# One-core attention and feed-forward kernel: the front recorded by the clocked loop with another load order, the tail in interleaved halves, the last key tile split, V products that may wait in the queue

## Chip, core and metric

The kernel runs on one core of one Trainium2 chip. The metric is the device time of one execution in microseconds. TensorE (PE), VectorE (DVE), ScalarE (ACT), GpSimd (POOL) and SyncE (SP) each take their instructions in order and meet at semaphores.

## What is computed

One token stream x of 2048 rows by 512 is normalised. Attention with 32 query heads of width 16 over one shared key and value head, and a feed-forward block of width 1792, both read the normalised rows; the second gates the first.

```python
xn = _layernorm(x, axis=-1)
q = (xn @ wq).reshape(B, S, 32, 16).transpose(0, 2, 1, 3)
k = xn @ wk
v = xn @ wv
p = softmax(einsum("bhqd,bkd->bhqk", q, k) * 16 ** -0.5)
s = einsum("bhqk,bkd->bhqd", p, v).transpose(0, 2, 1, 3).reshape(B, S, 512) @ wo
g = _silu(einsum("bsf,fd->bsd", _silu(xn @ w1), w2))
out = x + s * g
```

## The kernel before

Queries are cut into 4 chunks of 512, heads into 8 groups of 4: 32 groups, each against 16 key tiles of 128. One block is one head's scores of 512 queries against one key tile; a group has 64, all have 2048. `burst` (scores, L577) lets TensorE multiply blocks of a tile side by side in its row groups, from keys in `kTa_sb` for even groups and in `kTb_sb` for odd ones, where `move_K` (L430) copies them by DMA.

A block is exponentiated in one of two ways. Way A, `exp_A` (L606): two blocks stand in one of two PSUM buffers, `psA0` or `psA1`, and one ScalarE instruction takes both, 1024 columns. Way D, `exp_D` (L628): VectorE turns one bank (`D`, `D1` or `F`) into int16 bit patterns of an approximate exponential; when the four blocks of a tile are done, GpSimd adds two constants (L639), which gives three approximations of each block. So a block of way A needs one V product and one of way D three, with weighted copies of V (`vaug_sb`, L445). V products (`emit_PV`, L676) gather in the bank `psO`, four heads side by side. After a group's last one VectorE reads `psO` out with a transpose (`gn1`, L709), takes reciprocals of the sums (L717), scales (L726) and, every second group, transposes back (L736). Only then may the next group's V products write `psO`.

Dense work fills TensorE between score bursts: Q products, the feed-forward (`h` and `z`, whose ScalarE tanh is L882) and the output projection, with jobs planned over the run (L844). Weights are `w1_sb`, `w2_sb`, `wop_sb`.

The order is written by a recorder, `Sched`: each `op` gets its semaphore waits and advances a model of each engine's clock. From the thirteenth key tile on, a loop asks these clocks which instruction comes next: a score burst as late as ScalarE allows, V products or dense work ahead of it, filler matmuls (L865) where modelled TensorE activity is below `KEEP`. The front is written out by hand. For x tiles 0 to 3: statistics (L338), aggregates (L341), epsilon added (L352), Sqrt on ScalarE (L354), reciprocal (L355), the bias -mean x rstd (L359), normalisation on three engines (L366, L369), TensorE transposes and their evictions (L397 to L404), the first 128 keys (L412, L422), the Exp table (L484), Q of the first two groups (L454, L464), the other keys of chunk 0 (L424). Then 12 key tiles of group 0, all in way A, with the other three x chunks' work at fixed places (`dve_pre`, `pe_pre`); there rstd is taken on GpSimd by a power (L345, L347), and `warm` adds matmuls of zeros (L329). SyncE's queue issues most loads, K copies, x reloads and output stores; w1 and w2 are issued from GpSimd's (L323, L324).

The tail: the last four output tiles gather in `psA0` and `psA1` (L1163), first their share of the other groups by an identity matmul, then the last pair of groups. VectorE gates two of them (L1176); ScalarE copies two (L1179), which VectorE gates (L1183); it adds x to each (L893), and four stores leave, three from SyncE's queue and one from ScalarE's.

Of the kernel before, what the change touches and what calls it, by code (L numbers as in the profile page):

```python
# [6 lines left out]
ALU = mybir.AluOpType  # L7
# [25 lines left out]
PSUM_KEYS = {"A0", "A1", "D", "D1", "O", "F"}  # L33
# [163 lines left out]
def bass_recurrent_scan__grouped_kv_mqa__dense_activation_silu__prompt_kernel(  # L197
# [30 lines left out]
    NWARM2 = 2  # L228
    NWARM3 = 2
    NFRONT = 12  # L230
    AGE2 = 12.0
    KEEP, ENDQ, ROUND, MAXJOB, AHEAD, Q_EARLY = 0.6, 12, 3.0, 2, 3, 0.20
    LEAD, LEAD_END, SLIP, AGE, AGE1, MARGIN = 3, 3, 0.15, 2.0, 1.2, 0.0
    NF, F_FROM, F_LEFT, F_LATE, DENSE_END, HOLD, F_BEHIND = 14, 0.05, 9, 3, 0.95, 10, 0

    with ExitStack() as es:
# [32 lines left out]
        nb_sb = sb("nb_sb", [P, NT], FP32)  # L269
# [23 lines left out]
        def load_x(a, b, queue="sp"):  # L293
            op(queue, lambda e: e.dma_start(x_sb[:, a:b, :], xv[:, a:b, :]), writes=[("x", t) for t in range(a, b)],
               lane=f"lx{a}", cost=2.0 if b - a == 1 else 5.0)
# [5 lines left out]
        op("sp", lambda e: e.dma_start(wkn_sb[:], A_wk.rearrange("(dc p) e -> p dc e", p=P)), writes=["wkn"], lane="lwk")  # L301
        load_x(4, 8)
        op("sp", lambda e: e.dma_start(wq_sb[:], A_wq.rearrange("(dc p) n -> p dc n", p=P)), writes=["wq"], lane="lwq", cost=8.0)
        op("sp", lambda e: e.dma_start(wv_sb[:], A_wv.rearrange("(dc p) e -> p dc e", p=P)), writes=["wv"], lane="lwv")
# [6 lines left out]
        op("gp", lambda e: e.memset(mhalf_sb[:], -0.5), writes=["mhalf"])  # L311
        op("gp", lambda e: e.memset(scr_i[:], 0), writes=["scri"])
        op("v", lambda e: e.memset(zero_sb[:], 0.0), writes=["zero"])

# [5 lines left out]

        def late_loads():
            op("sp", lambda e: e.dma_start(wop_sb[:], A_wo.rearrange("(t p) n -> p t n", p=P)), writes=["wop"], lane="lwo")
            op("gp", lambda e: e.dma_start(w1_sb[:], B_w1.rearrange("(dc p) f -> p dc f", p=P)), writes=["w1"], lane="lw1")  # L323
            op("gp", lambda e: e.dma_start(w2_sb[:], B_w2.rearrange("(ft p) n -> p ft n", p=P)), writes=["w2"], lane="lw2")  # L324
# [12 lines left out]
        def stats(t):  # L337
            op("v", lambda e: e.bn_stats(stats_sb[:, t, :], x_sb[:, t, :]), reads=[("x", t)], writes=[("st", t)])  # L338

        def aggr(t):  # L340
            op("v", lambda e: e.bn_aggr(mv_sb[:, t, :], stats_sb[:, t, :]), reads=[("st", t)], writes=[("mv", t)])  # L341
# [8 lines left out]
        def rstd_sqrt(c):  # L350
            sl = slice(4 * c, 4 * c + 4)
            op("v", lambda e: e.tensor_scalar(rstd_sb[:, sl], mv_sb[:, sl, 1], LN_EPS, None, op0=ALU.add),  # L352
               reads=[("mv", t) for t in tiles(c)], writes=[("rstd", c)])
            op("a", lambda e: e.activation(rstd_sb[:, sl], rstd_sb[:, sl], ACT.Sqrt), reads=[("rstd", c)], writes=[("rstd", c)])  # L354
            op("v", lambda e: e.reciprocal(rstd_sb[:, sl], rstd_sb[:, sl]), reads=[("rstd", c)], writes=[("rstd", c)])  # L355

        def nbias(c):
            sl = slice(4 * c, 4 * c + 4)
            op("v", lambda e: e.scalar_tensor_tensor(out=nb_sb[:, sl], in0=mv_sb[:, sl, 0], scalar=-1.0, in1=rstd_sb[:, sl],  # L359
                                                     op0=ALU.mult, op1=ALU.mult),  # L360
               reads=[("mv", t) for t in tiles(c)] + [("rstd", c)], writes=[("nb", c)])

        def normalise(t, eng):
            rd = [("x", t), ("rstd", t // 4), ("nb", t // 4)]
            if eng == "a":
                op("a", lambda e: e.activation(xn_sb[:, t % 8, :], x_sb[:, t, :], ACT.Identity, bias=nb_sb[:, t:t + 1],  # L366
                                               scale=rstd_sb[:, t:t + 1]), reads=rd, writes=[("xn", t % 8)])
# [856 lines left out]
```

## Time and profile before

| what | us |
|---|---|
| median of three runs (683.57 to 683.84) | 683.79 |
| the profiled execution | 684.74 |
| its span, first to last instruction | 682.9 |
| first exponential of way A starts | 11.84 |
| last one ends | 673.68 |
| last group of V products (start and length) | 673.74, 0.40 |
| ScalarE, VectorE, TensorE busy | 665.0, 589.6, 640.3 |

The span is that of the profiled execution, not of the median run; what lies outside it is 1.8 us. Times in the trace count from the span's start. A row of the timeline merges equal instructions without a gap: its start, its length, their number, and in brackets the idle time before it with what ended that. Rows of a windows view give a stretch, its length, the busy time of PE, PE's weight loads, DVE, ACT and POOL with the number of instructions, then the granted TensorE clock as a share of full speed, the DMA share and GB/s.

### The profile page before, as it was taken

The numbers are of one execution on the slowest core, as the hardware profiler recorded it, in microseconds if no ns is written. First come the engines' busy times: TensorE is split into PE (matmuls) and PEld (weight loads), VectorE is DVE, ScalarE is ACT, GpSimd is POOL, SyncE is SP. The second block draws the span as 40 slices with busy tenths as digits, with TensorE's granted clock in tenths as the row PEclk, the third lists the DMA queues.
The fourth block names the chain that finished last, engine by engine and source line by source line (L and its number), as shares of the span: only waits on it lengthen the run. The fifth ranks groups of instructions, "written<-read, shape, count | busy, mean of one in ns | idle before, by whom it ended". The sixth has DMA issues, their size and how long they took to land.

```text
span 682.9 us, 14794 instructions
## 1 busy us (share of the span) xinstructions
PE 640.3 (94%) x6224; PEld 185.9 (27%) x6303; DVE 589.6 (86%) x976; ACT 665.0 (97%) x759; POOL 369.3 (54%) x375
## 2 busy tenths in 40 slices
PE   8999999999999999999999999999999999999986
PEld 3432222222222222222222222222222222222222
DVE  7788888779898889988888898998898989889985
ACT  5999999999999999999999999999999999999995
POOL 5134554456565556465564565556555556756553
PEclk9999999999999999999999999999999999999999
DMA  8310000000000001000000000000000000000100
GB/s 296 119 36 1 1 2 1 1 1 2 1 1 1 2 16 32 16 3 1 1 1 2 2 1 1 17 17 16 18 1 1 1 1 2 1 2 16 48 1 32
DMA packets 10194, 12.25 MB, mean 18 GB/s; under 512 B 2000, under 2 KB 9424, under 8 KB 10128
## 3 DMA queue, kind: packets, MB, share of 16 engines
q1 hardware_dynamic: 8960, 7.25, 3.6%
q0 software_dynamic: 736, 3.67, 1.5%
q8 instruction: 49, 0.80, 0.5%
q10 hardware_dynamic: 432, 0.39, 0.2%
q14 instruction: 17, 0.14, 0.1%
HBM read 8.95 MB, written 2.10 MB: 16 GB/s over the span
## 4 chain that ended last, share of the span: by engine, by line
ACT 88%; PE 7%; DVE 3%; DMA 0%; POOL 0%; issue 0%; DVEq 0%
ACT pa_sb L606 83%; ACT t_sb L882 5%; PE psA L577 2%; PE psO L676 2%; DVE stats_sb L338 1%; PE psF L844 1%; PE psF L329 0%; DVE ph_sb L628 0%; DMA x_sb<-in_A_x_dram 0%; PE psD L377 0%; DVE xn_sb L369 0%; POOL rstd_sb L347 0%; PE psD L412 0%; PE psF L412 0%; DVE kTa_sb L424 0%
## 5 line engine op out<-in xcount | busy, mean ns | idle before, releaser
L606 ACT ACTIVATE pa_sb<-psA 128x1024 bf16<-128x1024 f32 x678 | 644.4, 1189 | 3.9 <-PE psA L577 2.0
L639 POOL INT64_ADD ph_sb<-ph_sb x260 | 268.7, 1046 | 214.6 <-DVE ph_sb L628 214.6
L628 DVE TENSOR_SCALAR ph_sb<-psD 128x512 int16<-128x512 f32 (+1 forms) x464 | 321.9, 703 | 49.8 <-PE psD L577 41.3
L676 PE MATMUL psO<-ph_sb,vaug_sb 128*32 128x512 bf16 x1560 | 204.0, 385 | 0.4 <-ACT pa_sb L606 0.2
L676 PE MATMUL psO<-pa_sb,vaug_sb 128*32 128x512 bf16 x1356 | 202.9, 385 | 0.6 <-DVE vaug_sb L445 0.3
L577 PE MATMUL psA<-qT_sb,kTa_sb 32*128 32x512 bf16 x692 | 134.2, 384 | 10.2 <-ACT pa_sb L606 7.0
L577 PE MATMUL psA<-qT_sb,kTb_sb 32*128 32x512 bf16 x664 | 129.2, 386 | 11.8 <-ACT pa_sb L606 9.8
L639 POOL INT64_ADD x_sb<-x_sb x86 | 89.0, 1047 | 63.1 <-DVE x_sb L628 63.1
L577 PE MATMUL psD<-qT_sb,kTb_sb 32*128 32x512 bf16 x327 | 120.1, 386 | 0.4 <-DVE ph_sb L628 0.4
L628 DVE TENSOR_SCALAR x_sb<-psD 128x512 int16<-128x512 f32 (+1 forms) x149 | 104.0, 702 | 15.2 <-PE psD L577 14.0
L577 PE MATMUL psD<-qT_sb,kTa_sb 32*128 32x512 bf16 x309 | 112.0, 384 | 0.0
L676 PE MATMUL psO<-x_sb,vaug_sb 128*32 128x512 bf16 x516 | 92.9, 386 | 0.1
L577 PEld LDWEIGHTS psA<-qT_sb,kTa_sb 32*128 32x128 bf16 x692 | 32.5, 91 | 141.8 <-ACT pa_sb L606 129.0
L577 PEld LDWEIGHTS psA<-qT_sb,kTb_sb 32*128 32x128 bf16 x664 | 31.2, 91 | 144.5 <-ACT pa_sb L606 132.9
L676 PEld LDWEIGHTS psO<-ph_sb,vaug_sb 128*32 128x32 bf16 x1560 | 51.7, 95 | 50.7 <-issue 33.1
L844 PE MATMUL psF<-xnT_sb,w_sb 128*128 128x512 bf16 x194 | 60.9, 384 | 3.9 <-issue 2.4
L844 PE MATMUL psF<-w_sb,u_sb 128*128 128x512 bf16 x205 | 61.3, 383 | 2.5 <-issue 1.9
L676 PEld LDWEIGHTS psO<-pa_sb,vaug_sb 128*32 128x32 bf16 x1356 | 50.8, 94 | 45.2 <-issue 30.1
L882 ACT ACTIVATE t_sb<-psF 128x512 bf16<-128x512 f32 x72 | 55.2, 766 | 0.0
L914 DVE SCALAR_TENSOR_TENSOR u_sb<-t_sb,psF 128x512 bf16<-128x512 bf16 x56 | 38.3, 683 | 8.3 <-ACT t_sb L882 7.8
L577 PEld LDWEIGHTS psD<-qT_sb,kTb_sb 32*128 32x128 bf16 x327 | 28.3, 91 | 0.9 <-DVE ph_sb L628 0.7
L676 PEld LDWEIGHTS psO<-x_sb,vaug_sb 128*32 128x32 bf16 x516 | 23.1, 95 | 16.0 <-issue 11.2
(98 smaller groups left out, 361.1 us busy)
## 6 DMA issues: line engine op xcount, KB each, us to landing
w_sb<-in_B_w_dram POOLq DMA_DIRECT2D x2, 1792.0 KB, 12.3
x_sb<-in_A_x_dram SPq DMA_DIRECT2D x18, 128.0 KB, 2.3
out_dram<-ob_sb SPq DMA_DIRECT2D x15, 128.0 KB, 1.7
x_sb<-in_A_x_dram SPq DMA_DIRECT2D x3, 512.0 KB, 6.9
wq_sb<-in_A_wq_dram SPq DMA_DIRECT2D x1, 512.0 KB, 6.4
wop_sb<-in_A_wo_dram SPq DMA_DIRECT2D x1, 512.0 KB, 10.1
x_sb<-in_A_x_dram ACTq DMA_DIRECT2D x2, 128.0 KB, 3.1
kTb_sb<-kTa_sb SPq DMA_DIRECT2D x16, 16.0 KB, 2.9
```

Source lines behind the costliest of these rows:

```text
L338: op("v", lambda e: e.bn_stats(stats_sb[:, t, :], x_sb[:, t, :]), reads=[("x", t)], writes=[("st", t)])
L577: return e.matmul(ap, lhsT=kT_sb[g % 2][32 * i:32 * i + 32, kt * P:(kt + 1) * P], rhs=qT_sb[32 * i:32 * i + 32, c % 2, g // 2, :], start=T ...
L606: d = op("a", lambda e: e.activation(pa_sb[:, sl, :], psA[k][:, :], ACT.Exp, scale=ESCALE), reads=["A%d" % k], writes=[("pa", sl)], cost=2 ...
L628: d = op("v", lambda e: e.tensor_scalar(ph_ap(0, sl, 512 * pos, 512 * pos + m), src, float(PH_ONE + PH_BIAS), 0.0, op0=ALU.add, op1=ALU.ma ...
L639: d = op("gp", lambda e, j=j: e.int64_add(ph_ap(j, sl, 0, 2048).bitcast(I64), ph_ap(0, sl, 0, 2048).bitcast(I64), PH_SHIFT[j] * 0x00010001 ...
L676: r = e.matmul(psO[32 * i:32 * i + 32, :], lhsT=vaug_sb[:, p["v"], p["kt"], :], rhs=p["ap"], start=s0, stop=s1, tile_position=(0, 32 * i), ...
L844: h = e.matmul(ap, lhsT=l, rhs=r, start=(m == 0), stop=(m == end))
L882: op("a", lambda e: e.activation(t_sb[:, n % 2, :], bank_ap(b), ACT.Tanh, scale=0.5 if jb[0] == "h" else 0.25), reads=[b], writes=[("t", n ...
L914: op("v", lambda e: e.scalar_tensor_tensor(out=dst, in0=t_sb[:, n % 2, :], scalar=1.0, in1=src, op0=ALU.add, op1=ALU.mult), reads=tk["read ...
```

## The change

- Front: Sqrt takes epsilon as its bias, the Exp table is loaded right behind it, normalisation subtracts the mean itself and runs on VectorE alone. Evictions of the first transposes alternate between VectorE and ScalarE. First Q is computed in four pieces of 128 columns, evicted in two of 256 on ScalarE. The first 128 columns of wq have a load of their own, ahead of x tiles 4 to 7; w1 and w2 are loaded from SyncE's queue, w1 behind the K copies of chunk 0, w2 behind those of chunk 3.
- The hand-written list of 12 tiles is gone. Statistics, aggregates, normalisations become tasks of VectorE in the loop; transposes, K and V products of the x chunks become front jobs, which the loop places when their inputs are modelled ready and a bank is free. Way D may start for group 1 while the front runs. The three ph buffers and the one in x tiles are chosen by which is free.
- V products of a group may be queued up to `PVWAIT` before the modelled end of the last group's readout.
- In the last group one key tile is split: two of its blocks go way A, two way D, whose two additions run on VectorE.
- Tail: readout, reciprocal, scaling and back transpose run in halves of 256 columns, one half behind the other; each of the four output tiles has its own key. TensorE adds x and the gated product for tiles 0 and 2 in `psD`; ScalarE copies and stores them.

```diff
--- before
+++ after
-    NWARM2 = 2
+    NWARM2 = 0
...
-    LEAD, LEAD_END, SLIP, AGE, AGE1, MARGIN = 3, 3, 0.15, 2.0, 1.2, 0.0
+    LEAD, LEAD_END, SLIP, AGE, AGE1, MARGIN = 3, 3, 0.2, 2.0, 1.2, 0.0
+    HALF_LO, HALF_HI = 1, 3
+    EV = "vava"
+    PVWAIT = 0.2
...
+        wqv = A_wq.rearrange("(dc p) n -> p dc n", p=P)
+        op("sp", lambda e: e.dma_start(wq_sb[:, :, 0:P], wqv[:, :, 0:P]), writes=["wq0"], lane="lwq0", cost=4.0)
         load_x(4, 8)
-        op("sp", lambda e: e.dma_start(wq_sb[:], A_wq.rearrange("(dc p) n -> p dc n", p=P)), writes=["wq"], lane="lwq", cost=8.0)
-        op("sp", lambda e: e.dma_start(wv_sb[:], A_wv.rearrange("(dc p) e -> p dc e", p=P)), writes=["wv"], lane="lwv")
+        op("sp", lambda e: e.dma_start(wq_sb[:, :, P:D], wqv[:, :, P:D]), writes=["wq"], lane="lwq", cost=5.0)
+        op("sp", lambda e: e.dma_start(wv_sb[:], A_wv.rearrange("(dc p) e -> p dc e", p=P)), writes=["wv"], lane="lwv", cost=5.0)
...
+        def load_w1():
+            op("sp", lambda e: e.dma_start(w1_sb[:], B_w1.rearrange("(dc p) f -> p dc f", p=P)), writes=["w1"], lane="lw1", cost=7.0)
+
         def late_loads():
-            op("sp", lambda e: e.dma_start(wop_sb[:], A_wo.rearrange("(t p) n -> p t n", p=P)), writes=["wop"], lane="lwo")
-            op("gp", lambda e: e.dma_start(w1_sb[:], B_w1.rearrange("(dc p) f -> p dc f", p=P)), writes=["w1"], lane="lw1")
-            op("gp", lambda e: e.dma_start(w2_sb[:], B_w2.rearrange("(ft p) n -> p ft n", p=P)), writes=["w2"], lane="lw2")
+            op("sp", lambda e: e.dma_start(wop_sb[:], A_wo.rearrange("(t p) n -> p t n", p=P)), writes=["wop"], lane="lwo", cost=4.0)
+            op("sp", lambda e: e.dma_start(w2_sb[:], B_w2.rearrange("(ft p) n -> p ft n", p=P)), writes=["w2"], lane="lw2", cost=9.0)
...
-            op("v", lambda e: e.tensor_scalar(rstd_sb[:, sl], mv_sb[:, sl, 1], LN_EPS, None, op0=ALU.add),
-               reads=[("mv", t) for t in tiles(c)], writes=[("rstd", c)])
-            op("a", lambda e: e.activation(rstd_sb[:, sl], rstd_sb[:, sl], ACT.Sqrt), reads=[("rstd", c)], writes=[("rstd", c)])
-            op("v", lambda e: e.reciprocal(rstd_sb[:, sl], rstd_sb[:, sl]), reads=[("rstd", c)], writes=[("rstd", c)])
-
-        def nbias(c):
-            sl = slice(4 * c, 4 * c + 4)
-            op("v", lambda e: e.scalar_tensor_tensor(out=nb_sb[:, sl], in0=mv_sb[:, sl, 0], scalar=-1.0, in1=rstd_sb[:, sl],
-                                                     op0=ALU.mult, op1=ALU.mult),
-               reads=[("mv", t) for t in tiles(c)] + [("rstd", c)], writes=[("nb", c)])
+            op("a", lambda e: e.activation(rstd_sb[:, sl], mv_sb[:, sl, 1], ACT.Sqrt, bias=eps_sb[:, 0:1]),
+               reads=[("mv", t) for t in tiles(c)] + ["eps"], writes=[("rstd", c)], cost=4)
+            op("a", lambda e: e.activation(scr_sb[:, 0:1], mhalf_sb[:, 0:1], ACT.Exp), reads=["mhalf"], writes=["scr"], cost=4)
+            K.act_end += 1.28
+            op("v", lambda e: e.reciprocal(rstd_sb[:, sl], rstd_sb[:, sl]), reads=[("rstd", c)], writes=[("rstd", c)], cost=0.2)
 
         def normalise(t, eng):
+            op(eng, lambda e: e.tensor_scalar(xn_sb[:, t % 8, :], x_sb[:, t, :], mv_sb[:, t, 0:1], rstd_sb[:, t:t + 1],
+                                              op0=ALU.subtract, op1=ALU.mult),
+               reads=[("x", t), ("mv", t), ("rstd", t // 4)], writes=[("xn", t % 8)], cost=0.41)
...
+        def first_Q(ts, bank, key):
+
+            for n, t in enumerate(ts):
+                def f(e, n=n, t=t):
+                    for dc in range(NDC):
+                        r = e.matmul(bank[:, n * P:(n + 1) * P], lhsT=wq_sb[:, dc, 0:P], rhs=xnT_sb[:, dc, t * P:(t + 1) * P],
+                                     start=(dc == 0), stop=(dc == NDC - 1))
+                    return r
+                op("pe", f, reads=[("xnT", 0, t), "wq0"], writes=[key], cost=("full", [None] * NDC, P))
+
+        def first_evac_Q(a, b, bank, key, eng):
+            dst, src = qT_sb[:, 0, 0, a * P:b * P], bank[:, 0:(b - a) * P]
+            wr = ["qTb" if a else ("qT", 0, 0)]
...
-        normalise(0, "v")
-        normalise(1, "a")
-        normalise(2, "v")
-        normalise(3, "gp")
-        first_T(0, psD[:, 0:NQ], "D", "a")
-        first_T(1, psD[:, NQ:2 * NQ], "D1", "a")
-        first_T(3, psA[0][:, 0:NQ], "A0", "v")
-        first_T(2, psO[:, :], "O", "v")
-        mm_K(0, psA[1], "A1", 0, P)
-        evac_K(0, psA[1], "A1", 0, P, ["first"], "a")
-        op("a", lambda e: e.activation(scr_sb[:, 0:1], rstd_sb[:, 0:1], ACT.Exp), reads=[("rstd", 0)], writes=["scr"])
-        stats(4)
-        warm(NWARM2, psF[:, :], "F")
-        mm_Q(0, 0)
+        for t in tiles(0):
+            normalise(t, "v")
+        first_T(0, psD[:, 0:NQ], "D", EV[0])
+        first_T(1, psD[:, NQ:2 * NQ], "D1", EV[1])
+        first_T(2, psO[:, :], "O", EV[2])
+        first_T(3, psA[0][:, 0:NQ], "A0", EV[3])
...
+        for t in range(4, 4 + ST_EARLY):
+            stats(t)
+        first_Q((0, 1), psF, "F")
+        first_Q((2, 3), psD, "D")
+        first_evac_Q(0, 2, psF, "F", "a")
+        first_evac_Q(2, 4, psD, "D", "a" if Q_ACT else "v")
+        for t in range(4 + ST_EARLY, 8):
+            stats(t)
+        for t in range(4, 8):
+            aggr(t)
+        rstd_pow(1)
         mm_K(0, psO, "O", P, NQ)
-        evac_Q(0, 0, "v")
-
-
+        evac_K(0, psO, "O", P, NQ, [0, 1])
+        move_K(0)
+        load_w1()
...
+        def shift(tile, idx):
+            sl, n = slot_of[idx], len(rows_of[idx])
+            for j in range(1, NPH):
+                if n < 4:
+                    d = op("v", lambda e, j=j: e.tensor_scalar(ph_ap(j, sl, 0, NQ * n), ph_ap(0, sl, 0, NQ * n), float(PH_SHIFT[j]), None,
+                                                               op0=ALU.add),
+                           reads=[ph_key(0, sl, p) for p in range(n)], writes=[ph_key(j, sl, p) for p in range(n)], cost=0.4)
...
+        def vready(c, t):
+            return ("v", c) in tok and K.ready("pe", [("v", c)]) <= t + 0.1
 
         def emit_PV(t, cap):
             gi = state["g"]
             n = 0
-            if gi >= NGRP or t < gdone[gi]:
+            if gi >= NGRP or t < gdone[gi] - PVWAIT:
                 return 0
+            if t < gdone[gi]:
+                cap -= int((gdone[gi] - t) / 0.2163 + 0.7)
+                t = gdone[gi]
             while n < cap:
-                cand = sorted((p for p in pend[gi] if p["at"] <= t + 0.216 * n), key=lambda p: p["at"])
+                cand = sorted((p for p in pend[gi] if p["at"] <= t + 0.216 * n and vready(p["kt"] // 4, t)), key=lambda p: p["at"])
...
+            if owed[gi] == 0 and gi == NGRP - 1:
+                state["g"] += 1
...
+        def ln_ag(tk):
+            c = tk["c"]
+            for t in tiles(c):
+                aggr(t)
+            rstd_pow(c)
+            tok.add(("ag", c))
...
+        def front_ready(jb, t):
+            k, c = jb[:2]
+            if k == "T":
+                ts = [4 * c + 2 * jb[2] + n for n in range(2)]
+                return all(("nm", n) in tok for n in ts) and K.ready("pe", [("xn", n % 8) for n in ts]) <= t + 0.2
+            if k == "K":
+                return ("xnT",) + jb[1:] in tok and K.ready("pe", [("xnT",) + jb[1:]]) <= t + 0.2
+            return (c == 0 or all(("xnT", c, h) in tok for h in range(2))) and K.ready("pe", xnT_keys(c) + ["wv"]) <= t + 0.05
+
...
+        def next_half(t):
+
+            gi = NGRP - 1
+            if group_A() == gi and not shared and HALF_LO <= len(left[gi]) <= HALF_HI and free_slot(gi) is not None:
+                if kt_ready((gi, left[gi][-1]), t + SLIP):
+                    shared[(gi, left[gi][-1])] = [2, 3]
+                    return (gi, left[gi][-1])
+            return None
...
+                jb = next_front(t)
+                if jb and slots >= 2:
+                    b = free_banks(t + 0.04)
+                    if b:
+                        emit_front(jb, b[0])
+                        did = 2
+                can = job_ready(t) and not did
+                end = gi < NGRP and t >= gdone[gi] - PVWAIT and owed[gi] <= ENDQ
...
+        def resid(k, src, key, start):
+            b = "D1" if k else "D"
+            op("pe", lambda e: e.matmul(bank_ap(b), lhsT=ident[:, :], rhs=src, start=start, stop=not start), reads=["ident", key],
+               writes=[b], cost=("full", [None], NQ))
+
+        def store(k):
+            b = "D1" if k else "D"
+            op("a", lambda e: e.activation(ob_sb[:, k, :], bank_ap(b), ACT.Copy), reads=[b], writes=[("ob", k)])
+            op("a", lambda e, t=tt + k: e.dma_start(ov[:, t, :], ob_sb[:, k, :]), reads=[("ob", k)], writes=[("out", tt + k)], lane=f"st{k}a")
...
+        for k in (0, 2):
+            resid(k, x_sb[:, 12 + k, :], ("x", 12 + k), True)
+        warm(3, psF[:, :], "F")
...
+        for cs, h in half:
+            op("v", lambda e, cs=cs: e.transpose(otr_sb[:, sl, cs], psO[:, cs]), reads=["O"], writes=[("otr", sl) + h], cost=0.45)
+        for cs, h in half:
+            op("v", lambda e, cs=cs: e.reciprocal(rcp_sb[:, sl, cs.start // 32:cs.stop // 32],
+                                                  otr_sb[:, sl, cs].rearrange("p (a b) -> p a b", b=32)[:, :, DH]),
...
+        for cs, h in half:
+            op("v", lambda e, cs=cs: e.transpose(on_sb[:, slot, cs], onb_sb[:, so, cs]),
+               reads=[("onb", so, 0), ("onb", so, 1) + h], writes=[("xn", slot) + h], cost=0.45)
...
+        for k in (1, 3):
+            bank, key = tail_bank(k)
+            op("a", lambda e, k=k, bank=bank: e.activation(fint_sb[:, k, :], bank, ACT.Copy, scale=0.25), reads=[key],
+               writes=[("spart", k)])
+        gate(0)
+        gate(2)
+        for k in (0, 2):
+            resid(k, fint_sb[:, k, :], ("spart", k), False)
+            store(k)
+        for k in (1, 3):
+            gate_late(k)
+            final_add("v", tt + k, fint_sb[:, k, :], ("spart", k))
```

## Prediction

> **What bounds the kernel.** I read the page first: busy shares, the chain that ended last, the costliest groups.
>
> ```profile
> PE 640.3 (94%) x6224; PEld 185.9 (27%) x6303; DVE 589.6 (86%) x976; ACT 665.0 (97%) x759; POOL 369.3 (54%) x375
> ACT 88%; PE 7%; DVE 3%; DMA 0%; POOL 0%; issue 0%; DVEq 0%
> L606 ACT ACTIVATE pa_sb<-psA 128x1024 bf16<-128x1024 f32 x678 | 644.4, 1189 | 3.9 <-PE psA L577 2.0
> ```
>
> ScalarE sets the end: 97% busy, 88% of the chain. The chain's longest piece, 45 exponentials (L606) in 41.26 us, gives 0.917 us each. So the time has four terms: when the first exponential starts, how many there are, the gaps between them, and what follows the last. The timeline shows the first two thirds of the gaps:
>
> ```profile
> 7.13 1.12 DVE L369 TENSOR_SCALAR xn_sb<-x_sb,rstd_sb,nb_sb 128x512 bf16<-128x512 bf16 x2
> 8.04 1.08 ACT L402 ACTIVATE xnT_sb<-psD 128x512 bf16<-128x512 bf16 x2
> 9.42 1.28 ACT L484 ACT_TABLE_LOAD   x1
> 10.58 0.69 DVE L464 TENSOR_SCALAR qT_sb<-psF 128x512 bf16<-128x512 f32 x1 [0.56 <-PE psF L454]
> 11.84 2.85 ACT L606 ACTIVATE pa_sb<-psA 128x1024 bf16<-128x1024 f32 x3 [0.92 <-PE psA L577]
> 14.29 1.06 POOL L347 TENSOR_TENSOR rstd_sb<-rstd_sb,mhalf_sb 128x4 f32<-128x4 f32 x1
> 15.07 3.98 ACT L606 ACTIVATE pa_sb<-psA 128x1024 bf16<-128x1024 f32 x4 [0.37 <-PE psA L577]
> 19.38 4.01 ACT L606 ACTIVATE pa_sb<-psA 128x1024 bf16<-128x1024 f32 x4 [0.33 <-PE psA L577]
> 23.56 8.13 ACT L606 ACTIVATE pa_sb<-psA 128x1024 bf16<-128x1024 f32 x8 [0.17 <-PE psA L577]
> 31.85 20.80 ACT L606 ACTIVATE pa_sb<-psA 128x1024 bf16<-128x1024 f32 x22 [0.17 <-PE psA L577]
> ```
>
> The first 41 exponentials run from 11.84 to 52.65, 40.81 us. Without gaps they need 41 x 0.917 + 0.10 (a lone one takes 1.02) = 37.70. So 3.11 us are lost here, always to late scores (L577). From there to 617 one more gap costs 0.48, at 219. The end:
>
> ```profile
> 617.03 45.45 ACT L606 ACTIVATE pa_sb<-psA 128x1024 bf16<-128x1024 f32 x49
> 662.97 1.02 ACT L606 ACTIVATE pa_sb<-psA 128x1024 bf16<-128x1024 f32 x1 [0.49 <-PE psD L577]
> 664.29 9.39 ACT L606 ACTIVATE pa_sb<-psA 128x1024 bf16<-128x1024 f32 x10 [0.30 <-PE psF L577]
> ```
>
> ```profile
> 656.55:659.97 3.42, 2.21 (x25) 0.75 (x29) 3.42 (x7) 3.42 (x5) 2.33 (x3) 1.00 0.00 0
> 659.97:663.38 3.41, 3.41 (x30) 0.63 (x32) 1.80 (x4) 2.79 (x4) 2.15 (x2) 0.50 0.00 0
> ```
>
> 60 exponentials take 56.65 us, against 60 x 0.917 + 0.10 + 0.18 (start behind a tanh) = 55.3: 1.37 lost. The windows show why: TensorE ran at half clock (0.50) from 659.97 to 663.38, after a stretch in which it was busy only 2.21 of 3.42 us. The tail, then:
>
> ```profile
> 674.19 0.72 DVE L709 STREAM_TRANSPOSE otr_sb<-psO 128x512 f32<-128x512 f32 x1 [3.83 <-PE psO L676]
> 675.69 0.71 DVE L736 STREAM_TRANSPOSE xn_sb<-onb_sb 128x512 bf16<-128x512 bf16 x1
> 677.30 1.23 DVE L1176 SCALAR_TENSOR_TENSOR wq_sb<-psA,tmp_sb 128x1024 bf16<-128x1024 f32 x1 [0.90 <-PE psA L1163]
> 679.01 2.07 SPq L895 DMA_DIRECT2D out_dram<-ob_sb  x3
> 679.96 0.76 DVE L893 TENSOR_TENSOR ob_sb<-wq_sb,x_sb 128x512 bf16<-128x512 bf16 x2
> ```
>
> The last exponential ends at 673.68, the last V product at 674.13, the span at 682.94: 8.8 us of mostly serial VectorE work.
>
> **The change, part by part.** *Start.* Mean subtraction goes into the normalisation and epsilon into the Sqrt, so L352 (0.17) and L359 (0.16) leave the chain. Aggregates end at 6.25; Sqrt (0.20) to 6.49, reciprocal (0.18) to 6.70, normalisation from 6.73 instead of 7.13. Four on VectorE at 0.345 (the later row of four takes 1.38) end at 8.17. The last transposes (0.39) end at 8.61, their ScalarE eviction (0.59) at 9.25, the first K eviction (0.28) at 9.53. The Exp table load (1.28) now lies behind the Sqrt, where ScalarE idles. Two ScalarE evictions of 256 columns for Q are not in the trace: between 0.28 (128 columns, L422) and 0.59 (512, L402); I take 0.38, ending at 10.29. Scores (0.39) let the first exponential start at 10.78: **-1.06**. With Q evictions hidden it is 10.3, at 0.59 each and one more handoff 11.4. The Q columns needed first get a load of 128 KB of their own, between the 16 KB load (3.5 us to land) and the 512 KB one (6.4): it lands by 8.5, needed at 8.8, hidden; late, it costs its lateness one to one. Loads of x tiles 4 to 7 stand 128 KB further back and are needed at 8.9.
>
> *Front gaps.* The planned list becomes the clocked loop. I followed its built order by hand with these rows. The rest of K is evicted on VectorE behind four statistics (0.595 apart) and four aggregates (0.36), at 12.2: tile 1 loses 0.04, the burst behind three warm matmuls 0.15. Transposes and K products (0.62 each) between bursts cost 0.13, 0.11, 0.05. The second x chunk's normalisation waits for GpSimd (0.26 + 1.06): some 0.56, with the score burst queued behind the transposes on TensorE. Sum 1.04; I take 1.3 for what a hand misses, instead of 3.11: **-1.81**. Bounds 0.5 and 3.1 (one stall replaced by another). Weights w1 and w2 leave GpSimd's queue (issue 1.07 and 1.11 us) for SyncE's, w1 behind the first K copies, w2 behind the last; nothing on SyncE but K copies and x reloads stands behind them. The first tanh, which needs w1, comes at 52.45; w1 took 12.3 to land; hidden. Without that cover the next K copies wait behind 1.8 MB.
>
> *Count.* The built order has 677 exponentials, 72 tanh as before: half of the last key tile goes to VectorE. **-0.92**. VectorE gets two blocks (0.605) and two int16 additions of 1024, which no row shows: 0.41 (half as wide, L369) to 1.22 (L628 on 1024 from PSUM); I take 0.6. The last block should end 1.3 us before the last exponential does (scores two bursts earlier, VectorE with little to spare), the second addition 0.1 before: hidden. At 1.22 it ends 1.1 after and delays the last V products by 0.6.
>
> *End gap.* V products may stand in TensorE's queue up to 0.2 us before the accumulator psO is read out. Before, four score bursts ran without V products while the readout (657.35) waited behind VectorE's blocks; that is the thin stretch. The built order has two such bursts, so TensorE stays fuller and the half-clock stretch should not come: 0.3 left of 1.37, **-1.07**, between 0 and -1.37. At the other 30 group ends dense work already covers, so nothing; the loss if not is rival three.
>
> *Tail.* Three groups of V products come after the last exponential instead of one: **+0.44** (0.216 each). In halves the readout pays VectorE's fixed part eight times instead of four, but its handoffs vanish: 2.2 us both ways, the first half 0.35 earlier. Gates of 512 (0.69) replace one of 1024 (1.23); ScalarE copies (0.59) and stores two tiles whose residual TensorE added; VectorE gates and adds only two at the end (0.40 + 0.38 each). From the last V product: gates end at 3.8, ScalarE's second store is issued at 5.45, lands 1.7 later (row 6 of the page), 0.46 to the span's end: 7.6 instead of 8.77, **-1.12**; between -0.4 (ScalarE's queue, copies and store issue in turn, slower by two handoffs) and -1.6.
>
> Sum: -1.06 - 1.81 - 0.92 - 1.07 + 0.44 - 1.12 = -5.54. The profiled execution's 684.74 becomes 679.2. It lay 0.95 above the median of the runs, 683.79, so there 678.25: **678.3**.
>
> **Rivals.** *Gaps stay (0.17).* The loop's clock charges both GpSimd steps alike, the rows say 0.26 and 1.06; if VectorE falls behind, score bursts queue behind waiting transposes as before, and the thin stretch stays: 678.3 + 1.81 + 1.07 = 681.2. For it: every front gap ends on late scores. Against: the hand count gives a third.
>
> *Half clock in the front (0.10).* 48 warm matmuls become 40, and between 6.3 and 10.8 TensorE has transposes, 128-column products and waits. In 656.55 to 659.97, 2.21 busy of 3.42 was followed by half clock at 1.24 us of ScalarE gaps (1.37 less a later 0.12): 679.5. Against: in the front before, a like stretch did not trip it. [...]
>
> *Waiting V products block scores (0.11), slower.* At each of 31 group ends a V product at the head of TensorE's queue waits for the readout, and the score burst queues behind it. A score issued at 657.71 ended 0.4 before ScalarE needed it, so lateness decides from 0.2 + 0.4 us on. With 0.25 beyond that at each, 7.75: 686.0. For: the last readout began 1.3 us after its last V product. Against: from 53 to 617 gaps total 0.48, so the recorded order keeps time to within that slack.
>
> **Numbers.** Forecast 0.62, rivals 0.10, 0.17, 0.11. A difference under 0.2% (1.4 us) can't be told from no change. Faster: 0.62 + 0.10 + most of 0.17 = 0.86; same 0.03 (the rest of it); slower 0.11. The forecast's own range is 676.6 to 680.3 (bounds do not all fall on one side); to hold 8 in 10 the range reaches over the first rival: 676.6 to 682.4.
>
> **What would show it.** First exponential at 10.8; gaps to its 41st of about 1.3; 677 exponentials; no half clock near 660; last V product 0.9 after the last exponential; 7.6 from there to the end. Wrong, if ScalarE idles at group ends between 53 and 617, or the start stays above 11.5.

## The result and the profile after

The changed kernel takes 679.63 us (median of 6 runs, 679.32 to 679.89), the kernel before, run beside it, 683.82 (683.57 to 686.46). The ratio is 0.9932, 95% interval 0.9917 to 0.9947: faster, by 4.2 us or 0.7%. The forecast was 678.3 in a range of 676.6 to 682.4. The profiled execution took 679.43 us, span 677.6. (Of 58 executions with the new front, here and below, three, one each of `no_half`, `old_tail` and `no_wait_fill`, ran 10 to 13 us longer at a lower clock and are left out of the medians.)

From the page of the changed kernel: busy shares, the shares of the chain by engine, and the group of the exponentials.

```profile
PE 637.9 (94%) x6232; PEld 186.8 (28%) x6311; DVE 594.2 (88%) x994; ACT 664.0 (98%) x762; POOL 366.6 (54%) x371
ACT 89%; PE 4%; DVE 4%; issue 1%; POOL 1%; DMA 0%; POOLq 0%; SPq 0%
L560 ACT ACTIVATE pa_sb<-psA 128x1024 bf16<-128x1024 f32 x677 | 641.2, 1177 | 1.7 <-PE psA L531 1.2
```

ScalarE still sets the end, with 677 exponentials instead of 678. Its timeline (start, length, engine, line, tile, count, and in brackets the idle time before with its releaser) shows the front:

```profile
6.41 1.28 ACT L362 ACT_TABLE_LOAD   x1
9.29 0.38 ACT L462 ACTIVATE qT_sb<-psF 128x256 bf16<-128x256 f32 x1
9.74 0.38 ACT L462 ACTIVATE qT_sb<-psD 128x256 bf16<-128x256 f32 x1
10.72 3.77 ACT L560 ACTIVATE pa_sb<-psA 128x1024 bf16<-128x1024 f32 x4 [0.59 <-PE psA L531]
14.67 7.44 ACT L560 ACTIVATE pa_sb<-psA 128x1024 bf16<-128x1024 f32 x8 [0.18 <-PE psA L531]
22.57 14.08 ACT L560 ACTIVATE pa_sb<-psA 128x1024 bf16<-128x1024 f32 x15 [0.46 <-PE psA L531]
```

The table load stands ahead of the evictions, the first exponential comes at 10.72 instead of 11.84, and three gaps are left in the front: 0.28, 0.57 and 0.22 by the distance between the ends of exponentials, 1.07 in all instead of 3.10. (The exponential that starts at 22.57 ends at 23.6; below, its gap is called the gap at 23.6, and the first one the gap at 15.7.) At 22.57 the releaser is TensorE, but the row of VectorE's timeline ahead of it says who was late, and GpSimd's row by how much:

```profile
20.80 1.38 DVE L367 TENSOR_SCALAR xn_sb<-x_sb,mv_sb,rstd_sb 128x512 bf16<-128x512 bf16 x4 [0.30 <-POOL rstd_sb L355]
```

```profile
19.42 0.23 POOL L353 TENSOR_SCALAR rstd_sb<-mv_sb 128x4 f32<-128x4 f32 x1 [6.57 <-DVE mv_sb L349]
19.73 1.03 POOL L355 TENSOR_TENSOR rstd_sb<-rstd_sb,mhalf_sb 128x4 f32<-128x4 f32 x1
```

The end, in ScalarE's timeline: 59 exponentials in one piece (59 x 0.917 + 0.10 is 54.2), where the profile before had three pieces and 1.36 us of gaps. TensorE's window there (busy time of PE, PEld, DVE, ACT, POOL, then the granted clock) never falls to half clock:

```profile
614.16 54.38 ACT L560 ACTIVATE pa_sb<-psA 128x1024 bf16<-128x1024 f32 x59
```

```profile
653.52:656.94 3.42, 2.57 (x33) 0.79 (x33) 3.42 (x7) 3.42 (x5) 2.50 (x3) 1.00 0.00 0
656.94:660.35 3.41, 3.41 (x47) 0.87 (x44) 3.41 (x5) 3.41 (x5) 2.15 (x2) 1.00 0.00 0
```

The last exponential ends at 668.54, the last V product at 669.78, the span at 677.6. Rows of the tail:

```profile
669.82 0.78 DVE L1264 STREAM_TRANSPOSE otr_sb<-psO 128x256 f32<-128x256 f32 x2 [0.73 <-PE psO L650]
671.13 0.76 DVE L1276 STREAM_TRANSPOSE xn_sb<-onb_sb 128x256 bf16<-128x256 bf16 x2
672.09 1.29 DVE L1283 SCALAR_TENSOR_TENSOR wq_sb<-psA,tmp_sb 128x512 bf16<-128x512 f32 x2 [0.19 <-PE psA L1241]
674.99 0.38 ACTq L1256 DMA_DIRECT2D out_dram<-ob_sb  x1
```

Profile against profile, in us: first exponential -1.13; front gaps -2.03; gaps between 50 and 600 us +0.28 (0.48 to 0.76); one exponential -0.92; end gaps -1.36; last exponential to last V product +0.79 (0.45 to 1.24); from there to the end -0.97. Sum -5.3, and 684.74 less 679.43 is 5.31. But the medians differ by only 4.2. What of the 5.3 does a usual execution not get?

### The profile page after: what moved, and what is told of

It reads as the page before. It is cut to its first block, busy times and chain, and to the rows that moved or that the text cites. A ratio compares the mean times of both kernels' runs of the same rounds, so it can differ in the third digit from the quotient of the medians.

```text
span 677.6 us, 14816 instructions
## 1 busy us (share of the span) xinstructions
PE 637.9 (94%) x6232; PEld 186.8 (28%) x6311; DVE 594.2 (88%) x994; ACT 664.0 (98%) x762; POOL 366.6 (54%) x371
## 4 chain that ended last, share of the span: by engine, by line
ACT 89%; PE 4%; DVE 4%; issue 1%; POOL 1%; DMA 0%; POOLq 0%; SPq 0%
ACT pa_sb L560 84%; ACT t_sb L939 5%; PE psA L531 1%; PE psO L650 1%; DVE stats_sb L346 1%; DVE ph_sb L582 1%; DVE xn_sb L367 1%; PE psF L901 1%; DMA x_sb<-in_A_x_dram 0%; POOL ph_sb L607 0%; POOL rstd_sb L355 0%; PE psD L378 0%; DVE kTa_sb L421 0%; DVE x_sb L582 0%; PE psD L531 0%
## 5 line engine op out<-in xcount | busy, mean ns | idle before, releaser
L607 POOL INT64_ADD ph_sb<-ph_sb x292 | 302.5, 1048 | 234.8 <-DVE ph_sb L582 234.7
L582 DVE TENSOR_SCALAR ph_sb<-psD 128x512 int16<-128x512 f32 x530 | 360.1, 690 | 52.4 <-PE psD L531 43.9
L650 PE MATMUL psO<-ph_sb,vaug_sb 128*32 128x512 bf16 x1758 | 211.7, 384 | 0.6 <-ACT pa_sb L560 0.3
L650 PE MATMUL psO<-pa_sb,vaug_sb 128*32 128x512 bf16 x1354 | 199.2, 384 | 0.0
L531 PE MATMUL psD<-qT_sb,kTa_sb 32*128 32x512 bf16 x314 | 116.9, 384 | 0.4 <-DVE ph_sb L582 0.4
L607 POOL INT64_ADD x_sb<-x_sb x54 | 55.7, 1044 | 41.8 <-DVE x_sb L582 41.8
L582 DVE TENSOR_SCALAR x_sb<-psD 128x512 int16<-128x512 f32 (+1 forms) x96 | 66.9, 700 | 12.4 <-PE psD L531 11.7
L650 PE MATMUL psO<-x_sb,vaug_sb 128*32 128x512 bf16 x324 | 55.6, 384 | 0.0
L582 DVE TENSOR_SCALAR ph_sb<-psF 128x512 int16<-128x512 f32 x48 | 32.4, 676 | 0.0
L531 PEld LDWEIGHTS psD<-qT_sb,kTa_sb 32*128 32x128 bf16 x314 | 27.6, 91 | 2.0 <-DVE ph_sb L582 1.5
```

The lines of the kernel that those rows point to most:

```text
L531: return e.matmul(ap, lhsT=kT_sb[g % 2][32 * i:32 * i + 32, kt * P:(kt + 1) * P], rhs=qT_sb[32 * i:32 * i + 32, c % 2, g // 2, :], start=T ...
L582: d = op("v", lambda e: e.tensor_scalar(ph_ap(0, sl, 512 * pos, 512 * pos + m), src, float(PH_ONE + PH_BIAS), 0.0, op0=ALU.add, op1=ALU.ma ...
L607: d = op("gp", lambda e, j=j: e.int64_add(ph_ap(j, sl, 0, 4 * NQ).bitcast(I64), ph_ap(0, sl, 0, 4 * NQ).bitcast(I64), PH_SHIFT[j] * 0x0001 ...
L650: r = e.matmul(psO[32 * i:32 * i + 32, :], lhsT=vaug_sb[:, p["v"], p["kt"], :], rhs=p["ap"], start=s0, stop=s1, tile_position=(0, 32 * i), ...
```

## The experiments

**Is the half clock always there?** The kernel before, unchanged.

> The kernel before, unchanged. Theory: the half-clock stretch at 660 in its first profile, worth 1.24 us of ScalarE gaps, is not in every execution, since whether the thin stretch trips the clock depends on where it falls; the medians carry none or little of it, and so the 1.07 us of the prediction's end gap were earned against the profiled execution alone. Then this profile shows gaps of 0.1 to 0.4 us after 617 us instead of 1.36, a mean clock of 1.000 or 0.999 instead of 0.996, and times of 683.5 to 683.9. Rival: the stretch is a fixed part of this order. Then this profile shows half clock within 5 us of 660 again, a mean clock near 0.996 in nearly every run, and some other thing made the first profiled execution 0.95 us longer than the median.

Median 684.33 (683.38 to 686.98, 12 runs). The profiled execution, 683.69, has no half clock before the tail, and ScalarE's timeline shows no gap at the end:

```profile
617.33 55.30 ACT L606 ACTIVATE pa_sb<-psA 128x1024 bf16<-128x1024 f32 x60
```

The theory held: the gaps are even smaller than the 0.1 to 0.4 it named. Six executions lie at 683.4 to 684.0, with mean clocks of 0.998 to 1.000 (called clean below), six at 684.7 to 687.0 with 0.994 to 0.998. So a median of the kernel before depends on how many of each it holds. Half clock need not be all of the difference: one stretch cost 1.3 us, and the three slowest executions, which have no profile, are about 3 us over the clean ones. The same order, cut into windows of 3.41 us (the length of the half-clock stretch, 659.97 to 663.38) at another phase:

```profile
654.86:658.27 3.41, 2.53 (x33) 0.70 (x30) 3.22 (x6) 3.41 (x5) 2.48 (x3) 1.00 0.00 0
658.27:661.68 3.41, 2.88 (x35) 0.71 (x32) 3.41 (x7) 3.41 (x5) 2.43 (x3) 1.00 0.00 0
```

Here the thin stretch is shared by two windows, 2.53 and 2.88 us busy, and nothing happens; in the first profile one window got 2.21, and the next ran at half clock. What the windows held is taken up at the end.

**The waiting V products alone, taken away and added.**

```diff
-    PVWAIT = 0.2                            # no_pv_wait: the changed kernel
+    PVWAIT = 0.0
-            if gi >= NGRP or t < gdone[gi]: # before_wait: the kernel before
+            if gi >= NGRP or t < gdone[gi] - 0.2:
...
+            if t < gdone[gi]:
+                cap -= int((gdone[gi] - t) / 0.2163 + 0.7)
+                t = gdone[gi]
...
```

> The changed kernel with V products that never wait for the readout of the accumulator. It keeps 677 exponentials; 1,600 rows of TensorE's order change, only from the first group end on. Theory of the prediction: the waiting V products keep TensorE full at the last group end; without them the thin stretch is there again, and with it, where the clock trips, 1.07 us: 679.9 to 680.7, with more than 0.5 us of gaps after 617 us. Rival: the order without waits is as good or better, since it leaves two V product groups after the last exponential instead of three and the order's late gap of 0.1 to 0.4 us goes; 679.0 to 679.5, no gap over 0.2 us after 617 us.

> The kernel before with one part of the change: V products may stand in TensorE's queue up to 0.2 us before the accumulator is read out. It keeps 678 exponentials. Theory: this part alone removes the half clock, which the kernel before has in some executions only (12 runs of it: 683.4 to 684.0 in six, 684.7 to 687.0 in six). Then no execution over 684.2, the fastest no faster than before's fastest, 683.3 to 683.9, and no half clock before the tail in the profile. Rival: the waiting products cost more than they save, 0.3 us or more at each of many group ends; 686 or more. A second rival: the spread of the kernel before comes from elsewhere; then again half of the executions over 684.5.

`no_pv_wait`: median 679.76, ratio 0.9931 (0.9914 to 0.9948), three executions at 679.07 to 679.26, three at 680.25 to 680.59. The profile is of one of the latter, with 1.26 us of gaps from the second of these windows on:

```profile
653.53:656.95 3.42, 2.13 (x25) 0.67 (x25) 3.42 (x7) 3.42 (x5) 2.41 (x3) 1.00 0.00 0
656.95:660.36 3.41, 3.41 (x29) 0.62 (x30) 2.80 (x5) 2.73 (x4) 2.15 (x2) 0.50 0.00 0
```

Both sides were half right. The waits do keep the clock up near the last group end, but they cost: without them the clean executions are 0.6 us faster than the changed kernel's (679.71, below), 0.36 of it at the last V product (0.88 after the last exponential instead of 1.24); where the other 0.2 lies is not shown. They insure, 0.6 against 1.3 in half of the executions.

`before_wait`: median 684.29 (683.15 to 686.01), ratio 0.9998 (0.9987 to 1.0009). The theory failed as put, since six of twelve executions are over 684.5 again, which was the sign of the second rival. The stretch at 656 is filled (no half clock there in its profile), but the order now has a thin stretch 14 us later, and that one trips:

```profile
669.96:673.37 3.41, 2.09 (x26) 0.54 (x24) 0.00 (x0) 3.33 (x4) 1.37 (x2) 1.00 0.00 0
673.37:676.79 3.42, 3.42 (x11) 1.12 (x12) 2.11 (x4) 0.00 (x0) 0.00 (x0) 0.50 0.00 0
```

Half clock falls on the tail there: 10.2 us from the last V product to the end instead of 8.8. So the waits as such do not keep the clock up.

The second rival was right in part too. In this profile the first exponential starts at 12.81, 0.97 later than in the first one, because the first Q product waits for the load of wq:

```profile
10.48 1.02 PE L454 MATMUL psF<-xnT_sb,wq_sb 128*128 128x512 bf16 x4 [0.87 <-DMA wq_sb<-in_A_wq_dram]
```

The load took 7.7 us to land here, 7.0 in `before_again` (a wait of 0.30, first exponential at 12.15) and 6.4 in the first profile (no wait). None of the eleven profiles of the new front, where the 128 columns needed first have their own load, shows a wait for wq; their first exponentials start at 10.68 to 11.07.

**Is the changed kernel safe, and can filling alone do it?** The first is the changed kernel again; the second is `no_pv_wait` with

```diff
-... + 0.216 * idle) < KEEP:
+... + 0.216 * idle) < (KEEP if state["g"] < NGRP - 2 else 0.75):
```

> The changed kernel, unchanged, beside the others of this call. Theory: the only windows of TensorE that trip the clock are those that hold about 2.2 us of matmuls or less in 3.41 (2.21 and 2.13 were followed by half clock, 2.53 and 2.57 were not), and the changed order has none of these at whatever phase the windows fall (the lowest stretch after the start holds 2.52). So none of its executions is slow by a half-clock stretch: all within 679.2 to 680.0. Rival: its runs were clean by luck of the phase; then some executions at 680.5 or more, like those of the order without waits.

> The kernel without waiting V products again, but from the second last group on the loop adds warm matmuls whenever TensorE's share over 3.4 us would fall under 0.75 instead of 0.6. 677 exponentials; the order changes only after 640 us. Theory: TensorE's share in a window is what halves the clock, not the waiting as such; with the thin stretch filled no execution has the half clock: all within 679.1 to 679.9, none in the 680.2 to 680.6 that half of the executions without waits had. Rival: the clock falls for another reason (the readout of the accumulator, the kind of matmul), and half of the executions are at 680.2 or more again.

`after_again`: 679.71 (679.52 to 679.86), as the theory had it. `no_wait_fill`: 680.13 to 680.60. By the times the rival's sign came (three of four at 680.27 or more); the mean clocks, 0.999 and 1.000 instead of the 0.996 and 0.997 of the halved executions of `no_pv_wait`, speak for the theory. The one profile, of the execution left out, has full clock from 41.73 to 686.85, with 0.34 us of gaps near the end and the last V product 1.37 after the last exponential. So filling seems to remove the half clock there too, but it costs about 1.2 us against the clean executions without it, where at most 0.8 was expected: no gain.

**The front, the split tile and the tail.** `front_alone` has PVWAIT = 0, the old tail and

```diff
-    HALF_LO, HALF_HI = 1, 3
+    HALF_LO, HALF_HI = 1, 0
```

`no_half` has this line alone, `old_tail` only the tail of the kernel before.

> The changed kernel's front with the rest as before: no waiting V products, last key tile whole, old tail. 678 exponentials like the kernel before. Theory: the front is worth what the two profiles show for it, 1.13 at the first exponential and 2.03 of gaps behind it, less 0.28 of new gaps between 150 and 490 us: 2.9 us. Against the clean executions of the kernel before, 683.3 to 683.9, that is 680.4 to 681.0 where the clock is not halved, and about 1.3 us more in the executions where it is (the thin stretch at the last group end is there). Rival: the new front hands work on that must be done later; then less than 2 us are left, 681.5 or more in the fastest executions.

> The changed kernel with the last key tile not split: 678 exponentials, and no int16 additions on VectorE. Theory: the split wins one exponential (0.92 us) and loses nearly as much behind it, because its second addition took 1.25 us beside GpSimd's last one and held the last V product: last exponential to last V product 1.24 us in the changed kernel, 0.45 in the kernel before. Here then 0.92 later at the last exponential, about 0.5 from there to the last V product, the time within 0.2 us of the changed kernel's 679.6. Rival, the prediction's own terms (0.92 won, 0.44 lost): 0.48 us slower, 680.1, or more.

> The changed kernel with the tail of the kernel before: readout, gate and residuals after the last V product in whole tiles, no residuals on TensorE, three stores on SyncE's queue and one on ScalarE's. The order up to the last V product stays. Theory: the interleaved halves are worth what the two profiles differ by from the last V product to the end of the span, 8.81 against 7.84, so 0.97 us: 680.6. Rival: the old tail is not slower by itself, and ran late in the kernel before for lack of something else (a late buffer, the clock); then less than 0.3 us slower, 679.6 to 679.9.

`front_alone`: two executions at 680.83 and 680.85, four at 682.06 to 682.37 (mean clock 0.995 to 0.997). The first two are 2.7 us under the mean of the clean executions of the kernel before beside them (683.57), within the expected 680.4 to 681.0; ratio 0.9962 (0.9948 to 0.9976). `no_half`: 679.83 (679.59 to 679.87), 678 exponentials, last V product 0.45 after the last: with the waits the split gives back all but 0.1 of its 0.92. `old_tail`: 680.72 (680.54 to 680.78), 1.0 slower than `after_again`, 8.83 from the last V product to the end; the new tail is worth what the two profiles say.

**What holds the last V product?** The last four of GpSimd's additions shortened.

```diff
-... e.int64_add(ph_ap(j, sl, 0, 4 * NQ).bitcast(I64), ...
+m = NQ if tile[0] == NGRP - 1 and len(left[tile[0]]) <= 4 else 4 * NQ
+... e.int64_add(ph_ap(j, sl, 0, m).bitcast(I64), ...
```

> The changed kernel with the last four of GpSimd's additions cut to the first 512 of their 2,048 values; the rest of these values is left out, so that part of the last tiles' weights is not computed. No engine's order changes. Theory: the split tile's second int16 addition took 1.25 us because VectorE stands until GpSimd's addition beside it ends; alone both take about 0.27 (what was left of each after GpSimd's ended: 669.09 less 668.815). Then both rows show 0.25 to 0.35, the last V product ends 0.5 to 0.9 after the last exponential instead of 1.24, and the time is 0.4 to 0.7 us less than the changed kernel's, 679.0 to 679.3. Rival: the addition of 1,024 int16 values is slow by itself, or waits for a free buffer; then 1.25 again, and the last V product 0.9 us or more after the last exponential.

VectorE's timeline, first of the changed kernel, then of `short_add`, the split tile's two additions together:

```profile
667.42 1.67 DVE L603 TENSOR_SCALAR ph_sb<-ph_sb 128x1024 int16<-128x1024 int16 x2
```

```profile
667.72 0.76 DVE L603 TENSOR_SCALAR ph_sb<-ph_sb 128x1024 int16<-128x1024 int16 x2
```

Singly they took 0.50 and 1.25 in the one, 0.43 and 0.42 in the other. The stall beside GpSimd is shown. Its price was overrated: the last V product still comes 1.09 after the last exponential, 0.15 sooner, and the time is 679.58 (679.04 to 679.62), where 679.0 to 679.3 was expected. The other 0.64 over the 0.45 of the kernel before is three more steps of TensorE. The split tile has two rows, so its last V products start in pairs (at 669.18 and 669.39), where four started together at 668.96, and each pair takes a whole step of 0.216. The last eight products take 0.82 us, one product's 0.39 and two more steps; with the group before them four steps stand behind the last exponential, where the prediction counted three. Without waiting V products (`no_pv_wait`) the same split tile leaves three steps and 0.88.

**What leaves the gap at 23.6?** GpSimd's two steps charged what they take, for the second chunk or for all.

```diff
-    ... writes=[("rstd", c)])
+    ... writes=[("rstd", c)], cost=0.26 if c == 1 else None)   # true_costs: 0.3, c in (1, 2, 3)
-    ... writes=[("rstd", c)])
+    ... writes=[("rstd", c)], cost=1.06 if c == 1 else None)   # and SLIP 0.2 -> 0.16
```

> The changed kernel, recorded with GpSimd's two steps for the second chunk charged 0.26 and 1.06 us instead of 0.4 each. 677 exponentials; VectorE takes one statistic of the next chunk before the normalisation that waits for GpSimd and one between, and little else moves. Theory: the 0.57 us gap at 23.6 stands because VectorE, with everything it could have done already recorded behind the wait, waits 0.30 for GpSimd and the transposes and scores wait behind it; charged rightly it shrinks to 0.3 or less: 679.2 to 679.5. Rival: GpSimd's latency itself is what is late, and filling VectorE's wait with other work moves nothing on the path, or makes the normalisation later: gap within 0.1 of 0.57 or over it, 679.6 or more.

> The changed kernel recorded with GpSimd's two steps of every chunk charged 0.30 and 1.06 us, and SLIP 0.16 instead of 0.20. The built order has 675 exponentials, two fewer than the changed kernel's, with waits and the split tile kept. Theory: the front gap at 23.6 goes (0.3 us) and two exponentials (1.83) go to VectorE, with up to 0.3 of new gaps: 677.5 to 678.2. Rival: VectorE, which takes four more blocks (2.4 us) and stands beside GpSimd's additions at unforeseen places, falls behind, and the blocks given to it come back as gaps of ScalarE: 679 or more, with over 1.5 us more gaps than the changed kernel's 1.83.

`gp_cost_1`: 678.82 (678.78 to 679.40), ratio 0.9921 (0.9908 to 0.9935). The gaps at 15.7 and 23.6 are gone; one of 0.45 has come at 27, from the next chunk, still charged wrongly: 0.75 in the front instead of 1.07. That explains 0.3 of the 0.9 gained; the profiled execution was the slowest, and the rest, by which the time is below the expected 679.2 to 679.5, is open. `true_costs`: 676.52 (676.48 to 676.60), ratio 0.9872 (0.9854 to 0.9891), below the expected range. ScalarE's timeline:

```profile
10.92 35.90 ACT L560 ACTIVATE pa_sb<-psA 128x1024 bf16<-128x1024 f32 x39 [0.59 <-PE psA L531]
```

39 exponentials without a gap (39 x 0.917 + 0.10 is 35.9). With 675 exponentials (-1.83) and 0.62 us of gaps in all instead of 1.83 (-1.21) this is 3.0 of the 3.2 us between the medians, 679.71 and 676.52. It beats both kernels. How much of the count is due to the costs and how much to SLIP was not separated.

**The last four steps.** `true_costs`, with incomplete groups of V products allowed at the very end.

```diff
-... len(quad) < 4 and owed[gi] > len(cand)
+... len(quad) < 4 and not (gi == NGRP - 1 and not left[gi]) and owed[gi] > len(cand)
```

> The kernel recorded with true costs, and in the last group, once all its tiles are begun, V products go out in pairs as they come ready and need not be complete groups of four. 675 exponentials; only the order of the last 16 V products changes. Theory: of the 1.24 us between the last exponential and the last V product, three steps of 0.216 are the split tile's products, which have two rows only and so take a step for two products; issued before the last exponential ends, one of these steps leaves the end: 0.9 to 1.05 us there, time 676.2 to 676.4. Rival: the last addition, which stands beside GpSimd until 0.55 us after the last exponential, holds the last product whatever the order; then 1.2 us again, 676.5.

676.64 (676.54 to 676.78): the rival was right. TensorE's timeline shows it waiting for the stalled addition:

```profile
665.35 0.39 PE L650 MATMUL psO<-ph_sb,vaug_sb 128*32 128x512 bf16 x2
666.28 0.39 PE L650 MATMUL psO<-ph_sb,vaug_sb 128*32 128x512 bf16 x2 [0.54 <-DVE ph_sb L603]
```

The last V product comes 1.33 after the last exponential. Stall and steps cover each other: taking away one alone wins 0.15 or nothing. Both together were not tried.

## Why the prediction was right, and where it failed

- *Start, -1.06:* measured -1.13. The two unknown evictions, taken at 0.38, took 0.38. Against the two other profiles of the old front it is -1.4 and -2.1 or so (12.15 and 12.81 against 10.72): the wq load, which the prediction treats as hidden in the new order, was a risk in the old one.
- *Front gaps, -1.81 with 1.3 left:* 1.07 left. The one large stall that was named, GpSimd's power step at some 0.56, came as 0.57, and `gp_cost_1`, where only the charge is changed, shows its cause to be the recorder's charge for it.
- *Count, -0.92:* as built; with what the split tile adds at the end, 0.1 of it is left (`no_half`).
- *End gap, -1.07:* the mechanism is right (full clock from 656.94 to 660.35, where the first profile before had 0.50 from 659.97 to 663.38), and here the prediction's one real error lies, in the step behind the sum: "It lay 0.95 above the median of the runs, 683.79, so there 678.25". The 0.95 was mostly the half-clock stretch itself, which the three executions behind that median can hardly have had: clean ones take 683.4 to 684.0. The sum takes the stretch out; taking the 0.95 off as well counts it twice. Against the profiled execution the sum gave 679.2, and the measurement was 679.43. The miss of 1.38 on the median is 0.95 from this step, 0.23 from the sum, and 0.20 by which the profiled execution after lies under its own median. That the sum came so close is in part luck: three terms won 0.6 more than forecast (0.07, 0.22 and 0.29), and three came out 0.8 worse (0.35, 0.15 and 0.28).
- *V products behind the last exponential, +0.44:* 0.79. The additions, "I take 0.6 ... hidden", were not hidden (0.15), and a step was missed (0.20).
- *Tail, -1.12:* -0.97, and 1.0 by `old_tail`.
- *Nothing between 50 and 600:* +0.28, which the sum did not have. It is the same in `no_pv_wait` (0.74 in all), so it is not the waits. The largest gap, 0.48 at 154, has a like one in the kernel before, 0.48 at 219; what is new is small gaps near 443, 445 and 484. Within 8 us before each of these L735 ran long beside GpSimd (1.22 us from 150.84, 1.26 from 437.94, 0.82 from 480.27, instead of 0.41; below), but no run took that away by itself, so the cause is not shown.
- *Rivals.* The gaps did not stay. Half clock in the front is rare, but it came: in the profile of `no_wait_fill`, whose front is the changed kernel's, TensorE ran at half clock from 14.43 for 27.31 us, and the gaps of the front add up to about 11 us, far more than the 1.24 that the prediction gave this rival:

```profile
11.02:14.43 3.41, 2.30 (x29) 1.08 (x29) 2.64 (x11) 3.36 (x4) 1.33 (x2) 1.00 0.09 29
14.43:17.84 3.41, 3.41 (x24) 1.88 (x21) 2.30 (x5) 2.13 (x3) 0.00 (x0) 0.50 0.54 107
```

No median here contains it, and none of 70 executions of the kernel before took over 687.0; whether the new front causes it is not shown. The waiting products did not block scores (the gaps between 50 and 600 are the same without them); they cost 0.6, of which 0.36 at the end, instead of 7.75 over the whole.

By parts, between clean executions: front 683.6 to 680.84; with tail and split tile 679.15 (`no_pv_wait`); with the waits 679.7, where in return none of eleven executions took over 679.9. What within the front (the load of wq, the chain to the first exponential, the loop) is worth how much was read from profiles and not run apart.

## What to carry to other kernels

A stretch of half clock in one profile need not be in the median: before a term is credited for removing it, a second execution must show it again, and the sum is made against one execution throughout. Where a program records its own order from costs, first check those costs against the trace: two of them, 0.4 charged for steps of 0.26 and 1.06, were part of a change worth 3.2 us, against 4.2 for the whole edit. A stall and a serial chain that end at the same moment have no price singly.

## What was not expected of the hardware

*Half clock followed single windows of 3.41 us, and their busy time alone does not tell which.* The half-clock stretch in the first profile before lasted 3.41 us. The long stretches of full clock lasted 655.36 (that profile), 651.95, 665.60, 669.01 or 672.43 us (the changed kernel's): 192, 191, 195, 196 and 197 times 3.4133, from a start that moved against the first exponential from profile to profile (7.2 us ahead of it in the first profile before, 5.7 in that of the changed kernel). Near the end, a window with 2.09, 2.13 or 2.21 us of matmuls was followed by half clock for one window, one with 2.53 or 2.57 was not. Busy time alone does not sort them: in the first profile before, the window 4.61 to 8.02 held 2.07 us and the clock stayed up, and so it did after 1.84 us in the tail of `front_alone` and 1.80 in that of `gp_cost_1`:

```profile
671.65:675.07 3.42, 1.80 (x7) 0.48 (x6) 3.03 (x7) 2.17 (x4) 0.00 (x0) 1.00 0.09 31
675.07:678.48 3.41, 0.00 (x0) 0.00 (x0) 0.00 (x0) 0.00 (x0) 0.19 (x1) 1.00 0.35 122
```

What sorts them in these traces is the shape of the products. The traces give a score product as `32*128`, a V product as `128*32` and the products of the tail as `128*128`, the largest shape. Let each product count as its step (0.216 us for 512 columns) times its shape's share of `128*128`, a quarter for the first two. Then the three windows above that were followed by half clock hold 1.15 (`before_wait`), 1.11 (`no_pv_wait`) and 1.17 us (the first profile before), although they are over 60% busy, and the one with 1.80 holds 1.38. Over all 2,749 windows at full clock in the fourteen profiles, every one with up to 1.21 was followed by half clock and every one from 1.37 on was not. (Four of the low windows, all in fronts, have the record of a filler's weight load without that of its matmul; with this matmul counted, one that was followed by half clock, the 2.30 above, holds 1.16 and the three others 1.4 to 1.6.) This is read from the traces afterwards; no run was made to test it, so it is not shown to be what the clock goes by.

*Two kinds of VectorE instruction took longer beside GpSimd's additions, the conversions from PSUM did not.* In the changed kernel's trace, L735 (two inputs in SBUF) took 0.41 us on average in 18 executions of it, and 0.88, up to 1.26, in the 13 that began while GpSimd was busy. The conversions from PSUM (L582) average 0.69 in both cases. Timeline of VectorE, then of GpSimd, where the largest gap (0.48) outside the front began:

```profile
150.84 1.22 DVE L735 TENSOR_TENSOR onb_sb<-otr_sb,rcp_sb 128x256 bf16<-128x256 f32 x1
```

```profile
149.73 2.06 POOL L607 INT64_ADD x_sb<-x_sb  x2 [2.22 <-DVE x_sb L582]
```

GpSimd's pair ends at 151.79, and VectorE's row 0.27 behind it. L735 took 1.22 us beside the addition above and 0.41 without, the split tile's addition 1.25 and 0.42 (`short_add`), and GpSimd's addition took 1.13 or 1.20 instead of 1.04 where a L735 had begun before it. The lengths are measured; what makes them is not shown.
